# Seven block products for eight in the second expert layer's input product, with the weight preparation issued by a slot-wise feeder

## The chip, the cores and the metric

One core of a Trainium2 chip. The metric is the device time of one execution in microseconds (us), as the median of several; lower is better. TensorE does the matrix products, VectorE, ScalarE and GpSimd the elementwise work; the profile calls them PE (PEld for its weight loads), DVE, ACT and POOL. SP issues the transfers.

## The reference, cut to what matters

Local attention gives 1536 tokens of 512 features, a gated expert layer follows, and then the second one, where the change is:

```python
def _moe_ref(x, w_gate, w_val, w_out, rms_g):
    xn = x / rms * rms_g
    g = xn @ w_gate
    return (g * sigmoid(g) * (xn @ w_val)) @ w_out      # 512 -> 1536 -> 512

def _moe2_ref(x, w_in, w_out, s, b):
    h = x @ w_in                                        # 512 -> 2048
    r = np.maximum(h, 0.0)
    g = s * (r * r) + b
    return (g @ w_out).astype(np.float32)               # 2048 -> 512
```

The weights come as float64.

## The kernel before, in words

Every product of the expert layers is made of three matmuls per block of 128 x 128 weights and 512 tokens: a number is held as a high part (rounded to the matmul's fp32r format) and a low part (the rest), and high x high, low x high and high x low are summed in one PSUM bank. `mm12` (L797) does this for one strip of 128 output features and one chunk of 512 tokens: four blocks of the 512 inputs, twelve matmuls. The tokens are three chunks, s = 0, 1, 2. `banks(*range(8))` deals out the eight PSUM banks in turn, so that a bank comes back eight allocations later.

A weight strip (a "unit", 128 x 512) passes four steps, `w_load`, `w_scale`, `w_bits` and `w_split` (L222 to L279). The load brings the float64 as two 32-bit words, three buffers deep. The scale (ACT, L234) and the three word steps (DVE, L243 to L245) make a float32 of the two words in a buffer `wa`, of which there are three. The split makes the high part on ACT (L258) and the low part on POOL (L262), in rings of six. `slot(part)` (L812) is called after each product: it runs what was put off by `after(d, ...)` (a list of functions per slot ahead), one entry of `extra`, and then `w_ahead`, which moves the weight steps on by `w_to`. `next_w` hands out the next unit and, if it isn't ready, pushes it through at once. The list `order` (L190 to L200) sets the order of the stages and with it that of the units.

The first layer already has a part done with seven products for eight, `pair` (L955): two strips of the hidden features at a time, the first two token chunks as the two columns of a 2 x 2 block matrix, the third chunk in the plain way. Its derived weight blocks are units that are None in the list, made by `w_sums` (L265) from the unit before on POOL.

In the second layer, `s3(m)` (L987) does one of 16 strips of w_in2 for three chunks: 36 matmuls; for each chunk ACT makes u = relu(h) (L997), DVE s*u*u into the bank (L998), ACT the high part with the bias (L832), DVE the low part (L833). `s4(g)` (L1002) multiplies four strips' results with four rows of w_out2: 12 tiles of 128 tokens, 12 matmuls each, added to the output on DVE (L1025; the first group is copied by ACT, L1023). The last group is sent out tile by tile. The output product of the first layer, `s2(2)` (L929), adds its sum to the earlier parts (L945) and splits the result into y (`two`, L829 and L830), which is the input of s3.

Of the kernel before, what the change touches and what calls it, by code (L numbers as in the profile page):

```python
# [20 lines left out]
NPAIR = NH // 2  # L21
# [37 lines left out]
def kernel(ctx: ExitStack, tc: tile.TileContext, q_t, k_t, v_w, v_t, w_gate, w_val, w_out, w_in2, w_out2, vecs, out):  # L59
# [11 lines left out]
    xnp = pool("xn", 2)  # L71
    rawp = pool("raw", 3)
    wap = pool("wa", 3)
# [41 lines left out]
    qc = [const.tile([128, NPAIR, 2, HQ], F32, name=f"q{i}") for i in range(QB)]  # L115
# [80 lines left out]
    for m in range(KF2):  # L196
        order.append(("s3", m))
        if m % 4 == 0 and m:
            order.append(("s4", m // 4 - 1))
    order.append(("s4", KF2 // 4 - 1))  # L200
    units = []
    for kind, m in order:
        if kind == "s1":
            units += [w_gate[m], w_val[m]]
        elif kind in ("gate", "val"):
            units.append((w_gate if kind == "gate" else w_val)[m])
        elif kind == "s2":
            units += [w_out[KD * m + i] for i in range(KD)]
        elif kind == "pair":
            for q in range(2):  # L210
                units += [w_out[KD + m - PAIRS[0] + q], None]
        elif kind == "s3":
            units.append(w_in2[m])
        else:
            units += [w_out2[4 * m + i] for i in range(4)]
    NU = len(units)
    raw_t, a_t, ready = {}, {}, {}
# [4 lines left out]
    def w_load(i):  # L222
        if units[i] is None:
            return
        t = rawp.tile([128, 512, 2], I32, tag="raw", name="raw")
        fetch(out=t.rearrange("p f c -> p (f c)"), in_=units[i].bitcast(I32))
        raw_t[i] = t

    def w_scale(i):
        if units[i] is None:  # L230
# [17 lines left out]
    def w_bits(i):  # L248
        if units[i] is None:
            return  # L250
        for op in w_ops(i):
            op()
# [12 lines left out]
    def w_sums(i):  # L265

        t = sums[i + 1] = wsp.tile([128, 4, 128], F32, tag="ws", name="ws")
        a = a_t[i].rearrange("p (b c) -> p b c", b=4)
        for o, x0, x1, op in ((t[:, 0], a[:, 2], a[:, 3], ALU.add), (t[:, 1], t[:, 0], a[:, 0], ALU.subtract),
                              (t[:, 2], a[:, 0], a[:, 2], ALU.subtract), (t[:, 3], a[:, 1], t[:, 1], ALU.subtract)):  # L270
            nc.gpsimd.tensor_tensor(out=o, in0=x0, in1=x1, op=op)

    def w_split(i):
        if units[i] is None:
            a_t[i] = sums.pop(i).rearrange("p b c -> p (b c)")
        elif i + 1 < NU and units[i + 1] is None:
            w_sums(i)
        w_high(i)
        w_low(i)  # L279
# [4 lines left out]

    def w_to(*ns):
        for j in (3, 2, 1, 0):
            top = min(ns[j], prog[j - 1] if j else NU)
            if j == 0:
                top = min(top, prog[2] + 3)
            elif j == 1:  # L290
                top = min(top, prog[3] + 3)
            elif j == 3:
                top = min(top, live[0] + 6)
            while prog[j] < top:
                steps[j](prog[j])
                prog[j] += 1

    def w_ahead(part):

        i = used[0]  # L300
        if part == 0:
            w_to(i + 8, i + 7, 0, i + 5)
        elif part == 1:
            w_to(i + 8, 0, i + 6, 0)

    def next_w(keep=0):
        i = used[0]
        live[0] = i - keep
        while i not in ready:
            w_to(i + 4, i + 2, i + 2, i + 1)  # L310
        used[0] += 1
        return ready.pop(i)
# [531 lines left out]
    def moe(x, ps_m):  # L844

        gs, y = {}, []
# [81 lines left out]

        def s2(g):  # L929
            last = g > 0  # L930
            if last:
                flush()
                for s in range(NSUB):
                    y.append(xyp.tile([128, 2, KD, SUB], F32, tag="xy", name="y"))
            for m in range(KD):
                w = next_w()
                for s in range(NSUB):
                    ps = ps_m()[:, 0:SUB]
                    mm12(ps, w, lambda kk, e: hs[4 * g + kk][:, s, e])
                    slot(s)  # L940
                    acc = yp[:, m, s]
                    if not last:
                        nc.scalar.activation(out=acc, in_=ps, func=AF.Copy)
                    else:
# [42 lines left out]
        def s3(m):  # L987
            if m == 0:
                flush()
            w = next_w()  # L990
            g = gs[m] = chunk()
            for s in range(NSUB):
                ps = ps_m()[:, 0:SUB]
                mm12(ps, w, lambda kk, e: y[s][:, e, kk])
                slot(s)
                u = steady_u()
                nc.scalar.activation(out=u, in_=ps, func=AF.Relu)  # L997
                after(0, lambda u=u, ps=ps: nc.vector.scalar_tensor_tensor(out=ps, in0=u, scalar=sbc[:, 0:1], in1=u, op0=ALU.mult, op1=ALU.mult))  # L998
                after(1, lambda ps=ps, g=g[:, s]: two(ps, (g[:, 0], g[:, 1]), bbc[:, 0:1]))
            yield  # L1000

        def s4(g):  # L1002
# [3 lines left out]
            ws = [next_w(j) for j in range(4)]  # L1006
            for t in range(NT):
                st, c = divmod(t * 128, SUB)
                ge = [gs[4 * g + e][:, st, :, c:c + 128] for e in range(4)]
                parts = 2 if last and t == NT - 1 else 1  # L1010
                for k in range(parts):
                    cs = slice(k * DM // parts, (k + 1) * DM // parts)
                    acc = ps_m()[:, cs]
                    for e in range(4):
                        gh = r(ge[e][:, 0])
                        nc.tensor.matmul(acc, gh, r(ws[e][0][:, cs]), start=e == 0, stop=False)  # L1016
                        nc.tensor.matmul(acc, gh, r(ws[e][1][:, cs]), start=False, stop=False)  # L1017
                    for e in range(4):
                        nc.tensor.matmul(acc, r(ge[e][:, 1]), r(ws[e][0][:, cs]), start=False, stop=e == 3)  # L1019
                    if k == 0:  # L1020
                        slot(t % NSUB)
                    if g == 0:
                        nc.scalar.activation(out=op[:, t, cs], in_=acc, func=AF.Copy)  # L1023
                    else:
                        nc.vector.tensor_tensor(out=op[:, t, cs], in0=acc, in1=op[:, t, cs], op=ALU.add)  # L1025
                    if last:
                        nc.sync.dma_start(out=out[t * 128:(t + 1) * 128, cs], in_=op[:, t, cs])
                yield

        for kind, m in order:  # L1030
            yield from {"s1": s1, "gate": gate_of, "val": val_of, "s2": s2, "pair": pair, "s3": s3, "s4": s4}[kind](m)
# [15 lines left out]
def _layout(q, k, v, moe_w_gate, moe_w_val, moe_w_out, moe_rms_g, moe2_w_in, moe2_w_out, moe2_s, moe2_b):  # L1047
# [29 lines left out]
    def strips(w):  # L1077
# [14 lines left out]
        "w_in2": c(strips(moe2_w_in)).reshape(KF2, 128, 512),  # L1092
# [25 lines left out]
```

## Time and profile before

| | us |
|---|---|
| median of 3 runs | 637.85 (637.02 to 638.58) |
| the profiled execution | 637.69 |
| its span | 635.9 |
| TensorE busy in the span | 621.4 (98%) |
| VectorE, ScalarE, GpSimd busy | 405.9, 272.4, 200.5 |

The span is what the hardware profiler recorded on the core; the execution's own time has a little around it. The rows of the trace give busy time, count and mean duration of groups of instructions by line of the kernel, with the idle time of the engine just before them. A matmul's row shows its way through the pipeline, in which the next one has already begun. The attention and the first products take some 125 us, the first layer's rest runs to 371 us, the second layer from there to 633.

### The profile page before, as it was taken

The numbers are of one execution on the slowest core, as the hardware profiler recorded it, in microseconds if no ns is written. First come the engines' busy times: TensorE is split into PE (matmuls) and PEld (weight loads), VectorE is DVE, ScalarE is ACT, GpSimd is POOL, SyncE is SP. The second block draws the span as 40 slices with busy tenths as digits, with TensorE's granted clock in tenths as the row PEclk, the third lists the DMA queues.
The fourth block names the chain that finished last, engine by engine and source line by source line (L and its number), as shares of the span: only waits on it lengthen the run. The fifth ranks groups of instructions, "written<-read, shape, count | busy, mean of one in ns | idle before, by whom it ended". The sixth has DMA issues, their size and how long they took to land.

```text
span 635.9 us, 9741 instructions
## 1 busy us (share of the span) xinstructions
PE 621.4 (98%) x3826; PEld 511.6 (80%) x3826; DVE 405.9 (64%) x748; ACT 272.4 (43%) x547; POOL 200.5 (32%) x213
## 2 busy tenths in 40 slices
PE   5999999999999999999999999999999999999998
PEld 3877788878888888878888888888888888888886
DVE  5699884236714795799876768850588457845532
ACT  2898974324433443413343345531553055304400
POOL 2266844403414754637731101100410031103000
DMA  8897230003501131132232221140222221110022
GB/s 283 289 312 228 85 101 2 0 1 113 185 1 33 39 127 35 37 102 95 66 99 67 68 66 39 61 133 0 67 68 68 65 66 67 62 38 1 1 99 101
DMA packets 17015, 53.55 MB, mean 84 GB/s; under 512 B 1905, under 2 KB 2161, under 8 KB 16969
## 3 DMA queue, kind: packets, MB, share of 16 engines
q1 hardware_dynamic: 16968, 52.92, 25.8%
q8 instruction: 30, 0.49, 0.3%
q14 instruction: 17, 0.13, 0.1%
HBM read 48.86 MB, written 3.15 MB: 82 GB/s over the span
## 4 chain that ended last, share of the span: by engine, by line
PE 91%; DVE 4%; DMA 3%; ACT 1%; issue 1%; POOL 1%; DVEq 0%; POOLq 0%
PE b L808 20%; PE b L804 20%; PE b L805 20%; PE b L1019 7%; PE b L1016 7%; PE b L1017 7%; PE b L600 2%; PE b L656 2%; PE b L637 2%; DMA hg<-in_k_t_dram 1%; PE b L350 1%; PE b L951 1%; PE b L952 1%; PE b L953 1%; DMA q<-in_q_t_dram 1%
## 5 line engine op out<-in xcount | busy, mean ns | idle before, releaser
L262 POOL TENSOR_TENSOR wl<-wa,wh 128x512 fp32r<-128x512 f32 x68 | 90.0, 1330 | 295.1 <-ACT wh L258 259.0
L804 PE MATMUL b<-x,wh 128*128 128x512 f32 x288 | 113.7, 395 | 0.9 <-DVE u L779 0.9
L805 PE MATMUL b<-x,wl 128*128 128x512 f32 x288 | 112.2, 390 | 0.0
L258 ACT ACTIVATE wh<-wa 128x512 fp32r<-128x512 f32 x68 | 41.4, 625 | 89.3 <-PE b L1019 45.5
L808 PE MATMUL b<-x,wh 128*128 128x512 f32 x288 | 77.9, 392 | 0.0
L1017 PE MATMUL b<-wl,hg 128*128 128x512 f32 (+1 forms) x196 | 75.1, 385 | 0.0
L1016 PE MATMUL b<-wh,hg 128*128 128x512 f32 (+1 forms) x196 | 75.1, 385 | 0.0
L804 PE MATMUL b<-y,wh 128*128 128x512 f32 x192 | 74.7, 389 | 0.0
L805 PE MATMUL b<-y,wl 128*128 128x512 f32 x192 | 74.7, 389 | 0.0
L998 DVE SCALAR_TENSOR_TENSOR b<-u,vec 128x512 f32<-128x512 f32 x48 | 50.7, 1056 | 35.6 <-ACT u L997 35.6
L804 PEld LDWEIGHTS b<-x,wh 128*128 128x128 f32 x288 | 54.1, 188 | 12.4 <-issue 1.3
L805 PEld LDWEIGHTS b<-x,wl 128*128 128x128 f32 x288 | 54.1, 188 | 10.7
L808 PEld LDWEIGHTS b<-x,wh 128*128 128x128 f32 x288 | 53.5, 188 | 11.0
L245 DVE SCALAR_TENSOR_TENSOR wa<-raw,wa 128x512 int32<-128x512 int32 x68 | 56.8, 835 | 2.1
L244 DVE SCALAR_TENSOR_TENSOR wa<-raw,wa 128x512 int32<-128x512 int32 x68 | 54.6, 803 | 2.1
L833 DVE SCALAR_TENSOR_TENSOR hg<-b,vec,hg 128x512 fp32r<-128x512 f32 x48 | 36.0, 749 | 28.1 <-ACT hg L832 28.1
L1025 DVE TENSOR_TENSOR part<-b,part 128x512 f32<-128x512 f32 (+1 forms) x37 | 24.4, 674 | 43.5 <-PE b L1019 43.5
L1019 PE MATMUL b<-wh,hg 128*128 128x512 f32 (+1 forms) x196 | 51.5, 385 | 0.0
L832 ACT ACTIVATE hg<-b,vec 128x512 fp32r<-128x512 f32 x48 | 33.0, 688 | 43.0 <-DVE b L998 43.0
L808 PE MATMUL b<-y,wh 128*128 128x512 f32 x192 | 51.3, 389 | 0.0
L234 ACT ACTIVATE wa<-raw 128x512 f32<-128x512 f32 x68 | 44.4, 662 | 7.9 <-POOL wl L262 7.6
L1016 PEld LDWEIGHTS b<-wh,hg 128*128 128x128 f32 x196 | 36.8, 188 | 7.3
(116 smaller groups left out, 1072.0 us busy)
## 6 DMA issues: line engine op xcount, KB each, us to landing
raw<-in_w_out_dram SPq DMA_DIRECT2D x28, 512.0 KB, 3.6
raw<-in_w_in_dram SPq DMA_DIRECT2D x16, 512.0 KB, 3.5
raw<-in_w_gate_dram SPq DMA_DIRECT2D x12, 512.0 KB, 4.5
raw<-in_w_val_dram SPq DMA_DIRECT2D x12, 512.0 KB, 4.1
hg<-in_k_t_dram SPq DMA_DIRECT2D x8, 400.0 KB, 5.5
vt<-in_v_t_dram SPq DMA_DIRECT2D x8, 400.0 KB, 4.1
part<-in_v_w_dram SPq DMA_DIRECT2D x6, 528.0 KB, 5.9
q<-in_q_t_dram SPq DMA_DIRECT2D x12, 256.0 KB, 5.1
```

The source lines that it names most:

```text
L234: nc.scalar.activation(out=a, in_=raw_t[i][:, :, 1].bitcast(F32), func=AF.Copy, scale=2.0 ** -112)
L244: lambda: nc.vector.scalar_tensor_tensor(out=ai, in0=hi, scalar=-0x80000000, in1=ai, op0=ALU.bitwise_and, op1=ALU.bitwise_or),
L245: lambda: nc.vector.scalar_tensor_tensor(out=ai, in0=lo, scalar=29, in1=ai, op0=ALU.logical_shift_right, op1=ALU.bitwise_or),
L258: nc.scalar.activation(out=r(h), in_=a_t[i], func=AF.Copy)
L262: nc.gpsimd.tensor_tensor(out=r(lo), in0=a_t.pop(i), in1=high[i], op=ALU.subtract)
L804: nc.tensor.matmul(ps, r(hi[:, kk * 128:(kk + 1) * 128]), xh, start=kk == 0, stop=False)
L805: nc.tensor.matmul(ps, r(lo[:, kk * 128:(kk + 1) * 128]), xh, start=False, stop=False)
L808: nc.tensor.matmul(ps, r(hi[:, kk * 128:(kk + 1) * 128]), r(act(kk, 1)), start=False, stop=kk == 3)
L998: after(0, lambda u=u, ps=ps: nc.vector.scalar_tensor_tensor(out=ps, in0=u, scalar=sbc[:, 0:1], in1=u, op0=ALU.mult, op1=ALU.mult))
L1016: nc.tensor.matmul(acc, gh, r(ws[e][0][:, cs]), start=e == 0, stop=False)
L1017: nc.tensor.matmul(acc, gh, r(ws[e][1][:, cs]), start=False, stop=False)
L1019: nc.tensor.matmul(acc, r(ge[e][:, 1]), r(ws[e][0][:, cs]), start=False, stop=e == 3)
```

## The change

The strips of the second layer's w_in2 are done in pairs (`two_of`), eight of them. The inputs of a pair are 2 x 2 blocks for each half k of the inputs: two blocks of 128 input features by two strips. The first two token chunks are the other 2 x 2 matrix, and seven products, each of 2 x 3 = 6 matmuls, take the place of eight; sums of the banks (m1 is kept, u2, u3 and v are partial sums in SBUF) give the four results. The third chunk is done as before, 12 matmuls a strip. The derived blocks of the weights are units of their own, each named by the unit it comes from, and made by `w_sums` on POOL; `w_in2` is laid out anew on the host. The derived blocks of the activations (t1 to t4, and b11, b21, b22) are made by `yblocks` during the last output product of the first layer, whose last strip takes the chunks in the order 2, 0, 1. The square reads its first factor from the bank; the third chunk's low part goes to POOL.

The output products take the third chunk's tiles first, and do two strips for four tiles and then the other two, in four banks, so that only half of the weights are needed at first. From the fifth value strip of the first layer on, `feed` takes the place of `w_to` in the slots: at most one unit moves on by each step in one slot, with six `wa` buffers; from the end of the first layer on, scale and word steps stop while a pair runs (`stop`), and go on from the second half of the third chunk's tiles.

```diff
+    qp = pool("q", 1)
-    wap = pool("wa", 3)
+    wap = pool("wa", 6)
...
-    for m in range(KF2):
-        order.append(("s3", m))
-        if m % 4 == 0 and m:
-            order.append(("s4", m // 4 - 1))
-    order.append(("s4", KF2 // 4 - 1))
+    for g in range(KF2 // 4):
+        order += [("two", 2 * g), ("two", 2 * g + 1), ("s4", g)]
...
+        elif kind == "two":
+            n = len(units)
+            units += [w_in2[2 * m], w_in2[2 * m + 1], n, n + 1]
...
+    def feed():
+
+        now[0] += 1
+        for j in (3, 2, 1, 0):
+            while prog[j] < (prog[j - 1] if j else NU) and derived[prog[j]] and j < 3:
+                prog[j] += 1
+            i = prog[j]
+            if i >= (prog[j - 1] if j else NU):
+                continue
+            if j == 3 and i >= live[0] + 6 or j == 0 and real[i + 1] > real[prog[2]] + 3 or j == 1 and real[i + 1] > real[prog[3]] + 6:
+                continue
+            if j == 1 and now[0] < at.get((0, i), 0) + 3 or j == 2 and now[0] < at.get((1, i), 0) + 1:
+                continue
+            if j in (1, 2) and i >= stop[0]:
+                continue
+            if j == 1 and now[0] < at.get((3, nth[real[i] - 6]), 0) + 2:
+                continue
+            steps[j](i)
+            at[j, i] = now[0]
+            prog[j] += 1
...
+            if m == KF - 8:
+                wide[0] = 1
...
+        def yblocks(m, s, u):
+            k, j = divmod(m, 2)
+
+            def split(n, a, eng, late=0):
+                d = YB[k, n]
+                after(late, lambda: nc.scalar.activation(out=r(d[0]), in_=a, func=AF.Copy))
+                after(late, lambda: eng.tensor_tensor(out=r(d[1]), in0=a, in1=d[0], op=ALU.subtract))
+
+            yf[j, s] = u
+            e = nc.gpsimd
+            if s == 0:
+                split(("b11", "b21")[j], u, nc.vector)
+            elif j == 0:
+                t1 = yf["t1"] = steady_u()
+                e.tensor_tensor(out=t1, in0=u, in1=yf[0, 0], op=ALU.subtract)
+                split("t1", t1, e, 1)
+            else:
+                t2 = steady_u()
+                e.tensor_tensor(out=t2, in0=u, in1=yf["t1"], op=ALU.subtract)
+                nc.vector.tensor_tensor(out=yf[0, 1], in0=u, in1=yf[0, 1], op=ALU.subtract)
+                e.tensor_tensor(out=yf[1, 0], in0=yf[1, 0], in1=t2, op=ALU.subtract)
+                split("b22", u, nc.vector)
+                split("t2", t2, nc.vector)
+                split("t3", yf[0, 1], e)
+                split("t4", yf[1, 0], e)
...
+            def prod(bank, w, b, n):
+                for k in range(2):
+                    d = YB[k, n]
+                    cs = slice(b * 128, b * 128 + 128)
+                    nc.tensor.matmul(bank, r(w[k][0][:, cs]), r(d[0]), start=k == 0, stop=False)
+                    nc.tensor.matmul(bank, r(w[k][1][:, cs]), r(d[0]), start=False, stop=False)
+                    nc.tensor.matmul(bank, r(w[k][0][:, cs]), r(d[1]), start=False, stop=k == 1)
...
+            def act2(i, s, a):
+                d = g[i][:, s]
                 u = steady_u()
+                nc.scalar.activation(out=u, in_=a, func=AF.Relu)
+                after(0, lambda: nc.vector.scalar_tensor_tensor(out=a, in0=a, scalar=sbc[:, 0:1], in1=u, op0=ALU.mult, op1=ALU.mult))
+                if s == 2:
+                    after(1, lambda: nc.scalar.activation(out=u, in_=a, func=AF.Identity, bias=bbc[:, 0:1]))
+                    after(1, lambda: nc.scalar.activation(out=r(d[:, 0]), in_=u, func=AF.Copy))
+                    after(2, lambda: nc.gpsimd.tensor_tensor(out=r(d[:, 1]), in0=u, in1=d[:, 0], op=ALU.subtract))
+                else:
+                    after(1, lambda: nc.scalar.activation(out=r(d[:, 0]), in_=a, func=AF.Identity, bias=bbc[:, 0:1]))
+                    after(2, lambda: nc.vector.scalar_tensor_tensor(out=r(d[:, 1]), in0=a, scalar=bbc[:, 0:1], in1=d[:, 0], op0=ALU.add, op1=ALU.subtract))
...
+                w, k, b = {"m1": (aw, 0, "b11"), "m2": (aw, 1, "b21"), "m4": (aw, 3, "t4"), "m6": (sw, 1, "t2"),
+                           "m5": (sw, 0, "t1"), "m7": (sw, 2, "t3"), "m3": (sw, 3, "b22")}[n]
...
+                if n == "m1":
+                    nc.scalar.activation(out=m1, in_=bank, func=AF.Copy)
+                elif n == "m2":
+                    add(bank, bank, m1)
+                    act2(0, 0, bank)
+                elif n == "m6":
+                    add(u2, bank, m1)
+                elif n == "m7":
+                    add(u3, bank, u2)
...
+            turn = 'm1 m2 0 1 m6 m7 m4 m5 m3' if p == 0 else '0 m1 m2 1 m6 m7 m4 m5 m3'
...
+            for t0 in (8, 0, 4):
...
+                accs = [ps_m()[:, cs] for _ in range(4)]
+                for h in range(2):
+                    if h and t0 == 8:
+                        ws += [next_w(2), next_w(3)]
+                        stop[0] = NU
+                    for n in range(4):
+                        mms(accs[n], t0 + n, (2 * h, 2 * h + 1), cs, h == 0, h == 1)
+                        if n % 2 or t0 == 8:
+                            slot(0)
+                        if h:
+                            put(accs[n], t0 + n, cs)
```

In `turn`, "0" and "1" are the third chunk's two strips, each followed by its `act2`. m4 and m5 add u3, m3 adds v (m5's bank plus u2), and each of the three is followed by `act2`. The last group's output tiles of the first two chunks are done one by one, and the very last in two halves, as before.

## Rows read from the trace of the kernel before

**Rows 1.** The page's first part: busy us (share of the span) and instructions

```profile
span 635.9 us, 9741 instructions
## 1 busy us (share of the span) xinstructions
PE 621.4 (98%) x3826; PEld 511.6 (80%) x3826; DVE 405.9 (64%) x748; ACT 272.4 (43%) x547; POOL 200.5 (32%) x213
```

**Rows 2.** TensorE's waits: line, releaser, us in total, times, longest us

```profile
PE b L804 <- DVE u L779: 0.9, 1, 0.9
...
PE b L951 <- DVE part L976: 0.3, 1, 0.3
```

**Rows 3.** Windows: length, busy us of PE, PEld, DVE, ACT, POOL, then PEclk, DMA

```profile
446.80:479.40 32.60, 32.60 (x146) 26.99 (x145) 22.74 (x31) 17.87 (x31) 8.92 (x7) 1.00 0.20 66
479.40:512.10 32.70, 32.70 (x146) 27.09 (x145) 19.66 (x30) 6.15 (x11) 2.92 (x3) 1.00 0.20 65
...
223.00:239.00 16.00, 16.00 (x73) 13.15 (x72) 14.43 (x22) 7.05 (x12) 8.74 (x10) 1.00 0.36 121
271.00:285.00 14.00, 13.73 (x61) 11.06 (x60) 13.79 (x23) 2.62 (x5) 3.96 (x3) 1.00 0.29 94
```

**Rows 4.** The chain in order of time, one strip: start us, us, what

```profile
446.88 0.91 PE b L808 x4
...
449.60 0.91 PE b L808 x4
```

**Rows 5.** Groups by line and shape: busy us, mean ns; second layer's strips, first layer's pairs

```profile
L804 PE MATMUL b<-y,wh 128*128 128x512 f32 x192 | 74.7, 389 | 0.0
...
L953 PE MATMUL b<-hg,wh 128*128 128x512 f32 x44 | 17.1, 389 | 0.0
```

**Rows 6.** The same view, VectorE: the operations on banks

```profile
L998 DVE SCALAR_TENSOR_TENSOR b<-u,vec 128x512 f32<-128x512 f32 x48 | 50.7, 1056 | 35.6 <-ACT u L997 35.6
...
L833 DVE SCALAR_TENSOR_TENSOR hg<-b,vec,hg 128x512 fp32r<-128x512 f32 x48 | 36.0, 749 | 28.1 <-ACT hg L832 28.1
...
L1025 DVE TENSOR_TENSOR part<-b,part 128x512 f32<-128x512 f32 x35 | 23.6, 688 | 41.7 <-PE b L1019 41.7
...
L945 DVE TENSOR_TENSOR b<-b,part 128x512 f32<-128x512 f32 x12 | 8.3, 696 | 2.8 <-PE b L808 2.8
...
L976 DVE TENSOR_TENSOR part<-b,part 128x512 f32<-128x512 f32 x16 | 10.4, 677 | 0.0
```

**Rows 7.** By line: duration ns min/median/max, first and last start, VectorE

```profile
L998 DVE SCALAR_TENSOR_TENSOR b<-u,vec x48: 748/752/1804, 375.0 to 602.0; 128x512 f32<-128x512 f32 x48
...
L244 DVE SCALAR_TENSOR_TENSOR wa<-raw,wa x68: 679/693/1667, 21.0 to 582.5; 128x512 int32<-128x512 int32 x68
...
L976 DVE TENSOR_TENSOR part<-b,part x16: 673/677/684, 223.5 to 289.2; 128x512 f32<-128x512 f32 x16
```

**Rows 8.** Groups by line and shape, ScalarE

```profile
L832 ACT ACTIVATE hg<-b,vec 128x512 fp32r<-128x512 f32 x48 | 33.0, 688 | 43.0 <-DVE b L998 43.0
```

**Rows 9.** Groups by line and shape, GpSimd, and one line's spread

```profile
L262 POOL TENSOR_TENSOR wl<-wa,wh 128x512 fp32r<-128x512 f32 x68 | 90.0, 1330 | 295.1 <-ACT wh L258 259.0 <-DVE b L945 19.4 <-PE b L1019 7.2
...
L271 POOL TENSOR_TENSOR ws<-wa 128x128 f32<-128x128 f32 x8 | 3.7, 463 | 3.4 <-DVE wa L245 3.4
...
L271 POOL TENSOR_TENSOR ws<-wa,ws 128x128 f32<-128x128 f32 x4 | 2.3, 573 | 0.0
...
L885 POOL TENSOR_TENSOR hg<-hg x8: 1288/1392/1744, 197.5 to 266.5; 128x512 fp32r<-128x512 f32 x8
```

**Rows 10.** Groups by line, VectorE, 371 to 600 us: the word steps

```profile
L244 DVE SCALAR_TENSOR_TENSOR wa<-raw,wa 128x512 int32<-128x512 int32 x26 | 18.0, 692 | 0.9
L245 DVE SCALAR_TENSOR_TENSOR wa<-raw,wa 128x512 int32<-128x512 int32 x26 | 18.0, 692 | 0.9
...
L243 DVE TENSOR_SCALAR wa<-wa 128x512 int32<-128x512 int32 x26 | 10.9, 420 | 0.0
```

More of the change, by code (lines that the diff above doesn't have):

```diff
@@ L114 @@
     junk = const.tile([128, DM], mybir.dt.bfloat16, name="junk")
-    qc = [const.tile([128, NPAIR, 2, HQ], F32, name=f"q{i}") for i in range(QB)]
+    qc = [qp.tile([128, NPAIR, 2, HQ], F32, tag=f"q{i}", name="q") for i in range(QB)]
     part = const.tile([128, 2 * VT], F32, name="part")
@@ L216 @@
     NU = len(units)
+    derived = [isinstance(u, int) for u in units]
+    real = [0]
+    for d in derived:
+        real.append(real[-1] + (not d))
     raw_t, a_t, ready = {}, {}, {}
@@ L222, in w_load @@
     def w_load(i):
-        if units[i] is None:
+        if derived[i]:
             return
@@ L229, in w_scale @@
     def w_scale(i):
-        if units[i] is None:
+        if derived[i]:
             return
@@ L248, in w_bits @@
     def w_bits(i):
-        if units[i] is None:
+        if derived[i]:
             return
@@ L263, in w_low, with w_sums @@
         ready[i] = (high.pop(i), lo)
-    def w_sums(i):
-        t = sums[i + 1] = wsp.tile([128, 4, 128], F32, tag="ws", name="ws")
+    def w_sums(i, of):
+        t = sums[of] = wsp.tile([128, 4, 128], F32, tag="ws", name="ws")
         a = a_t[i].rearrange("p (b c) -> p b c", b=4)
@@ L273, in w_split @@
     def w_split(i):
-        if units[i] is None:
+        if derived[i]:
             a_t[i] = sums.pop(i).rearrange("p b c -> p (b c)")
-        elif i + 1 < NU and units[i + 1] is None:
-            w_sums(i)
+        else:
+            for k in (i + 1, i + 2):
+                if k < NU and derived[k] and units[k] == i:
+                    w_sums(i, k)
         w_high(i)
@@ L283 @@
     live = [0]
+    wide = [0]
     def w_to(*ns):
@@ L287, in w_to @@
             top = min(ns[j], prog[j - 1] if j else NU)
[L288 to L293, printed above, removed]
-            while prog[j] < top:
-                steps[j](prog[j])
-                prog[j] += 1
+            while prog[j] < top:
+                i = prog[j]
+                if j == 0 and real[i + 1] > real[prog[2]] + 3 or j == 1 and real[i + 1] > real[prog[3]] + 3:
+                    break
+                if j == 3 and i >= live[0] + 6:
+                    break
+                steps[j](i)
+                prog[j] += 1
+    now, at, stop = [0], {}, [NU]
+    nth = [i for i in range(NU) if not derived[i]]
+    def feed():
[3 more added lines that the diff above has]
+                prog[j] += 1
+            i = prog[j]
+            if i >= (prog[j - 1] if j else NU):
[8 more added lines that the diff above has]
+                continue
+            steps[j](i)
+            at[j, i] = now[0]
+            prog[j] += 1
     def w_ahead(part):
         i = used[0]
-        if part == 0:
+        if wide[0]:
+            feed()
+        elif part == 0:
             w_to(i + 8, i + 7, 0, i + 5)
@@ L934, in s2 @@
                     y.append(xyp.tile([128, 2, KD, SUB], F32, tag="xy", name="y"))
+                room()
             for m in range(KD):
                 w = next_w()
-                for s in range(NSUB):
+                for s in (2, 0, 1) if last and m == KD - 1 else range(NSUB):
                     ps = ps_m()[:, 0:SUB]
                     mm12(ps, w, lambda kk, e: hs[4 * g + kk][:, s, e])
+                    if last and m == KD - 1 and s < 2:
+                        stop[0] = 0
                     slot(s)
@@ L1005, in s4, with mms @@
                 flush()
-            ws = [next_w(j) for j in range(4)]
-            for t in range(NT):
+            ws = [next_w(0), next_w(1)]
+            def mms(acc, t, es, cs, start, stop):
                 st, c = divmod(t * 128, SUB)
[L1009 to L1027, printed above, removed]
@@ new lines, in mms @@
+                ge = [C[e][:, st, :, c:c + 128] for e in es]
+                for n, e in enumerate(es):
+                    gh = r(ge[n][:, 0])
+                    nc.tensor.matmul(acc, gh, r(ws[e][0][:, cs]), start=start and n == 0, stop=False)
+                    nc.tensor.matmul(acc, gh, r(ws[e][1][:, cs]), start=False, stop=False)
+                for n, e in enumerate(es):
+                    nc.tensor.matmul(acc, r(ge[n][:, 1]), r(ws[e][0][:, cs]), start=False, stop=stop and n == len(es) - 1)
@@ L1028, in s4 @@
                 yield
         for kind, m in order:
-            yield from {"s1": s1, "gate": gate_of, "val": val_of, "s2": s2, "pair": pair, "s3": s3, "s4": s4}[kind](m)
+            yield from {"s1": s1, "gate": gate_of, "val": val_of, "s2": s2, "pair": pair, "two": two_of, "s4": s4}[kind](m)
     x = [xs0]
```

132 lines of the change are left out of this document (115 added, 17 removed).

## The prediction

> **What bounds the kernel now.** I read the page's busy times first: TensorE is busy 621.4 us of a 635.9 us span, VectorE 405.9, ScalarE 272.4, GpSimd 200.5 [rows 1]. A busy TensorE need not be a working one, so I went to TensorE's waits: apart from the attention at the start, only two products waited, 0.9 and 0.3 us [rows 2]. The windows show one strip stage and one output stage of the second expert layer: TensorE is busy for the whole 32.6 and 32.7 us at a granted clock of 1.00 (the 2.4 GHz level), VectorE for 22.74 and 19.66, GpSimd for 8.92 and 2.92 [rows 3]. So here TensorE is the bound, and every other engine has slack. The chain in order of time gives the unit price: the four closing matmuls of two successive twelves begin at 446.88 and 449.60, so 2.72 us for 12, or 0.2267 us each [rows 4]. The 389 ns of a matmul's own row [rows 5] is its length in the pipeline, with the next one already begun, and isn't the price.
>
> **What the change removes from TensorE.** Two strips cost 2 x 3 x 12 = 72 matmuls before. After, two token chunks go through seven products of 2 blocks x 3 terms (42 matmuls), the third through 2 x 12 = 24: 66 in all. That is 6 fewer per pair of strips and 48 fewer over eight pairs, 48 x 0.2267 = **10.88 us**. The output products keep 12 matmuls per tile, in another order. A six-matmul product on one bank is not new: the first layer's pairs run so at 389 ns each, and a stretch of them, 223 to 239 us, has TensorE busy throughout with 73 matmuls, 0.219 each [rows 3, 5]. So I take no cost for starting a bank more often (nine banks per pair where there were six).
>
> **What each pair adds, per 66 x 0.2267 = 14.96 us of TensorE.**
> - VectorE: six squares, four low parts, seven block sums. The square now reads its first factor from the bank, as the low part does, so I price it by that row, 0.749 us, and not by the old square's mean of 1.056 [rows 6]. Sums into a bank cost 0.696 (m2, m4, m5, m3), into SBUF 0.677 (m6, m7, and v): 10 x 0.749 + 4 x 0.696 + 3 x 0.677 = 12.3 us; they come densest from m6 to m3, and the next twelve-matmul product lets the engine catch up. Cover: 14.96 us of products and a ring of eight banks, in which each is wanted again eight products later. The dear end is the row of operations with both inputs in SBUF, which spread from 0.752 to 1.804 [rows 7]; that is the third rival. I take the cheap one, as a sum read from a bank (673 to 684 ns over 16, GpSimd at work among them [rows 7]) is the same instruction.
> - ScalarE: at most 19 operations (four high parts, six Relus, six biased copies, two more copies for the third chunk, one copy of m1); at the dearest row, 0.688 [rows 8], 13.1 us. It fits.
> - GpSimd: a weight block set costs three subtractions or sums of 0.463 and one of 0.573, 1.96 us, and a low part 1.330 [rows 9]. The first pair of each group of two does two sets, four low parts and the third chunk's two low parts: 3.9 + 5.3 + 2.7 = 11.9 us; the second does no set, 8.0. At the dearest GpSimd price, 1.744 [rows 9], the first pair makes 3.9 + 6 x 1.744 = 14.4 us, still under 14.96.
> - Nothing is added to the DMA: the derived blocks are computed, the strips are as many bytes as before, and the loads go through the same queue with the same three buffers.
>
> **What is moved.** The word steps, 0.420 + 0.692 + 0.692 = 1.80 us for a strip in the second layer [rows 10], leave the pairs for the output products. I walked the new feeder slot by slot: it lifts its stop after the first four of sixteen slots, does at most one unit in a slot, and gets all eight units through by the stage's last slots. VectorE then has 8 x 1.80 + 12 x 0.688 (adding a tile [rows 6]) = 22.7 us in 32.6, and what runs over is not wanted before the pair after next. The same walk gives the lead of each split weight: derived blocks are issued at the last two slots of an output stage and wanted after 8.2 us of products, against two high and two low parts, 4.0 us; the second half of an output stage's weights is issued at m4 and m5 and wanted 6.8 us after the last, against three low parts, 4.0 us. The units are always in place when asked for, so the emergency path is not taken. The feeder also takes over from the fifth value strip of the first layer on; no unit there is split less than one gate strip ahead. Zero for all of it; with the cover gone, a late weight costs TensorE at most its own 1.33 us low part each time.
>
> **The seam before the first pair.** The blocks t1 to t4 of the activations are made in the first layer's last output product. Only those of its last strip can be late. After its last matmul come a VectorE sum (0.7), two GpSimd subtractions and two GpSimd low parts one after the other; at 1.39 us, the middle of such an operation [rows 9], t4 is ready after 6.3 us, and t3 after 4.9. TensorE has m1, m2 and both third-chunk products in between, 8.2 us, before m6, and comes to t3 after 9.5 and to t4 after 10.9. Cost zero, up to the first rival's 1.5 us.
>
> **The sum.** The profiled execution took 637.69 us around its span of 635.9; the median of the three runs is 637.85, 0.16 above. 637.69 - 10.88 = 626.8, and from the median 627.0. I forecast **626.9 us**.
>
> **The rivals.**
> 1. Part is given back where GpSimd queues. In the seam a whole split unit may stand ahead (1.96 + 1.74), then four operations at 1.744, with 1.4 us of sum and copy: t4 at 12.1 us against 10.9, t3 at 10.3 against 9.5, so 1.2 us; and one low part (about 1 us) late in another place. It ends at 626.9 + 2.2 = **629.1 us**. For it: GpSimd has twice the work per pair that it has now. Against: its queue is empty through most of the second layer. Chance 0.12.
> 2. The word steps overrun the output products. Their two steps with both inputs in SBUF spread from 0.69 to 1.667 us [rows 7], and GpSimd works 2 x (1.96 + 1.33) + 2 x 1.33 = 9.2 us in that stage. If all of that holds VectorE up, it has 22.7 + 9.2 = 31.9 us to do in 32.6, with 27.2 left when the stop lifts, and carries up to 4.7 us into the next pair, which would then ask 17.0 of VectorE in 14.96: 2.0 us late after each of three output stages, **633 us**. Against: the late operations feed banks wanted eight products later. Chance 0.05. The Trainium skill (SBUF — State Buffer, Who interferes with whom) says that a VectorE instruction with two SBUF inputs and a GpSimd instruction that reads SBUF shut each other out, the loser for the whole instruction. By that rule this rival's 9.2 us would be lost in full, and a pair's sums, each with one input in a bank, would lose nothing; the spread of the word step and the steady sum agree with its direction [rows 7], the full blocking is not shown.
> 3. Slower: VectorE becomes the bound inside the pairs. If its operations there are held up as the old square was, mean over median 1.056 / 0.752 = 1.40 [rows 6, 7], a pair takes 12.3 x 1.40 = 17.2 us and TensorE waits for a bank. It decides from 16.32 us, what two strips took (72 x 0.2267), on: 8 x (17.2 - 16.32) = +7.0, **645 us**. For it: GpSimd is busy 8 to 12 us of each pair. And in the first layer's second pair, where sums and word steps meet, VectorE is busy for 13.79 of 14.00 us and TensorE loses 0.27 [rows 3]. Against: that stretch holds the word steps of three strips, which these pairs don't, and the sums themselves didn't stretch [rows 7]. Chance 0.04.
> 4. The product count falls and the time doesn't, because each bank begun costs something that the twelve-matmul products hide. Three more banks per pair would have to cost 0.45 us each to eat 1.36: **637.8 us**. The first layer's pairs speak against it [rows 3]. Chance 0.03.
>
> **How the numbers follow.** The forecast keeps 0.76. A measurement of this kernel can tell about 0.2% from no change: runs differ by 1.56 us, 0.25%. Faster by more than that: the forecast, rivals 1 and 2, 0.93; same: rival 4, 0.03; slower: rival 3, 0.04. The range goes down to 625.7, if the two waits of 1.2 us go as well, and up to 629.9, rival 1 with half the runs' spread (0.8) on top; that holds the forecast and rival 1, 0.88, less what an unlisted wait may take.
>
> **What would show it.** Right: TensorE busy all through the pairs, the ends of two pairs 14.96 us apart, VectorE near 12 us and GpSimd near 12 or 8 us in one, squares at 0.75 us, no word step inside a pair, about 48 fewer matmuls. Wrong: a wait of TensorE on a GpSimd low part at m6, m7 or m4 (rival 1), word steps in a pair (2), VectorE above 15 us there and TensorE waiting for it (3), or pairs over 15 us without a wait (4).

## The result, and the profile after

The changed kernel takes **628.62 us** (628.22 to 629.92, four runs) against 637.43 (636.58 to 638.58, four runs) for the kernel before: a ratio of 0.9864 [0.9842, 0.9887]. The forecast was 626.9, the range 625.7 to 629.9: the time lies inside it, 1.7 us above the forecast. The profiled execution took 628.22 us around a span of 626.3, 9.6 us less than before.

The page's first part, against [rows 1]:

```profile
span 626.3 us, 9872 instructions
## 1 busy us (share of the span) xinstructions
PE 610.6 (97%) x3778; PEld 502.2 (80%) x3778; DVE 447.7 (71%) x790; ACT 299.4 (48%) x593; POOL 301.9 (48%) x321
```

TensorE has 48 matmuls fewer and 10.8 us less to do (621.4 - 610.6). The three other engines have more: VectorE 41.8 us, ScalarE 27.0, GpSimd 101.4. Next, the windows of the second layer, to be read against [rows 3]: the first two pairs, an output product, two more pairs, an output product. The columns are the length, then the busy time of PE, PEld, VectorE, ScalarE and GpSimd, the granted clock and the DMA share.

```profile
372.80:387.80 15.00, 15.00 (x68) 12.43 (x67) 12.53 (x15) 9.88 (x17) 12.51 (x12) 1.00 0.00 0
387.80:402.80 15.00, 15.00 (x68) 12.43 (x67) 12.08 (x20) 10.77 (x19) 8.95 (x8) 1.00 0.00 1
402.80:435.40 32.60, 32.60 (x145) 27.00 (x145) 22.13 (x32) 16.21 (x28) 11.12 (x13) 1.00 0.42 129
435.40:450.40 15.00, 15.00 (x68) 12.43 (x67) 7.03 (x11) 8.88 (x15) 11.79 (x15) 1.00 0.01 2
450.40:465.30 14.90, 14.90 (x67) 12.33 (x67) 11.45 (x19) 10.92 (x19) 7.61 (x7) 1.00 0.00 0
465.30:497.90 32.60, 32.60 (x146) 27.00 (x145) 28.21 (x42) 10.67 (x18) 13.54 (x16) 1.00 0.36 114
```

TensorE never pauses; a pair takes the 14.96 us of the forecast, where two strips took 16.32. VectorE, with 12.5 us at most in a pair, has room to spare, and the word steps are in the output products (28.21 us of VectorE in 32.6). So the second layer did what was forecast. What was not forecast is in TensorE's waits, the columns as in [rows 2]; of the view, all that comes after the attention:

```profile
PE b L1039 <- DVE part L1064: 1.1, 1, 1.1
...
PE b L836 <- DVE u L811: 0.9, 1, 0.9
...
PE b L1039 <- DVE part L1054: 0.8, 1, 0.8
```

The 0.9 is the one of before. The 1.1 and the 0.8 are new, and they lie in the **first layer's** first pair of seven products (L1039 is L951 of before). They take the place of the 0.3 of [rows 2], which was in the second pair: by these rows 1.6 us more.

The rows of the waits understate it. A wait's row begins where the last matmul's own row ends, 0.39 us after its start, while the price of that matmul is 0.2267; so the cost of a stop is read from the starts. The first pair's first matmul, the last one ahead of the longer wait, and the first matmul behind the pair (start, us, engine, line, operation, tiles, count):

```profile
217.48 0.39 PE L1039 MATMUL b<-hg,wh 128*128 128x512 f32 x1
...
227.86 0.39 PE L1041 MATMUL b<-hg,wh 128*128 128x512 f32 x1
...
235.28 0.40 PE L836 MATMUL b<-x,wh 128*128 128x512 f32 x1
```

The pair's 66 matmuls take 17.80 us (217.48 to 235.28), where they took 14.98 in the kernel before (218.56 to 233.54) and would take 14.96 at the unit price. The second pair no longer loses anything: 14.96 us, where it took 15.52. The first layer is so 2.26 us longer by the starts (2.82 - 0.56). TensorE also came to the first pair 1.08 us earlier (217.48 against 218.56), which is less than the profiles of the changed kernel and of the runs below differ among themselves (216.98 to 219.72). -10.88 + 2.26 - 1.08 = -9.70 us, beside the -9.6 of the span.

The stretch around the pair, columns as in [rows 3], first of the kernel before, then of the changed one; the third line of each is the whole of it, in which 178 matmuls were begun before and 165 now:

```profile
200.00:216.00 16.00, 16.00 (x72) 13.27 (x71) 7.55 (x12) 7.25 (x13) 6.58 (x5) 1.00 0.11 34
216.00:236.00 20.00, 20.00 (x90) 16.48 (x89) 19.65 (x27) 8.22 (x14) 12.74 (x12) 1.00 0.26 82
200.00:240.00 40.00, 40.00 (x178) 33.05 (x177) 29.88 (x41) 17.18 (x30) 22.48 (x19) 1.00 0.21 66
```

```profile
200.00:216.00 16.00, 16.00 (x72) 13.25 (x71) 14.87 (x20) 7.18 (x13) 6.64 (x5) 1.00 0.42 133
216.00:236.00 20.00, 18.07 (x78) 13.93 (x77) 19.79 (x23) 9.29 (x17) 15.86 (x14) 1.00 0.29 93
200.00:240.00 40.00, 38.07 (x165) 30.50 (x164) 38.56 (x49) 16.46 (x29) 23.68 (x18) 1.00 0.32 106
```

Before, VectorE was already full in the second stretch (19.65 of 20) but half idle ahead of it, and so it came in without arrears. Now it has little room in either (14.87 of 16, 19.79 of 20): the feeder, which has six buffers to fill and starts just here, puts four sets of word steps into the first stretch (one before). VectorE enters the pair late. Its timeline there (start, us, engine, line, operation, tiles, count):

```profile
223.65 1.27 DVE L1054 TENSOR_TENSOR part<-b,part 128x512 f32<-128x512 f32 x2
224.85 0.41 DVE L246 TENSOR_SCALAR wa<-wa 128x512 int32<-128x512 int32 x1
225.29 1.68 DVE L247 SCALAR_TENSOR_TENSOR wa<-raw,wa 128x512 int32<-128x512 int32 x1
227.01 1.67 DVE L248 SCALAR_TENSOR_TENSOR wa<-raw,wa 128x512 int32<-128x512 int32 x1
228.59 2.47 DVE L1064 TENSOR_TENSOR part<-b,part 128x512 f32<-128x512 f32 x4
```

The bank that TensorE wants at 228.25 is released by the sums of L1064, and in the queue a set of word steps stands ahead of them, two of which take 1.7 us where [rows 10] have 0.69. Steps of that length are not new (before, three in this stretch took 1.66); their number ahead of the pair is. TensorE gets the bank at 229.33:

```profile
229.33 0.50 PE L1039 MATMUL b<-hg,wh 128*128 128x512 f32 x1 [1.08 <-DVE part L1064]
```

### The profile page after: what moved, and what is told of

The parts are those of the page before. It is cut to its first block, busy times and chain, and to the rows that moved or that the text cites. A ratio compares the mean times of both kernels' runs of the same rounds, so it can differ in the third digit from the quotient of the medians.

```text
span 626.3 us, 9872 instructions
## 1 busy us (share of the span) xinstructions
PE 610.6 (97%) x3778; PEld 502.2 (80%) x3778; DVE 447.7 (71%) x790; ACT 299.4 (48%) x593; POOL 301.9 (48%) x321
## 4 chain that ended last, share of the span: by engine, by line
PE 90%; DVE 4%; DMA 2%; issue 2%; ACT 1%; POOL 0%; DVEq 0%; POOLq 0%
PE b L840 13%; PE b L836 13%; PE b L837 13%; PE b L1198 7%; PE b L1195 7%; PE b L1196 7%; PE b L1123 5%; PE b L1099 4%; PE b L1097 4%; PE b L1098 4%; PE b L1125 2%; PE b L632 2%; PE b L688 2%; PE b L669 2%; DMA hg<-in_k_t_dram 1%
## 5 line engine op out<-in xcount | busy, mean ns | idle before, releaser
L1195 PE MATMUL b<-wh,hg 128*128 128x512 f32 (+1 forms) x196 | 75.1, 385 | 0.0
L247 DVE SCALAR_TENSOR_TENSOR wa<-raw,wa 128x512 int32<-128x512 int32 x68 | 64.0, 941 | 2.1
L248 DVE SCALAR_TENSOR_TENSOR wa<-raw,wa 128x512 int32<-128x512 int32 x68 | 60.4, 888 | 2.1
L1108 DVE SCALAR_TENSOR_TENSOR b<-b,vec,u 128x512 f32<-128x512 f32 x48 | 35.9, 758 | 35.5 <-ACT u L1107 35.3
L1198 PE MATMUL b<-wh,hg 128*128 128x512 f32 (+1 forms) x196 | 58.0, 385 | 0.0
L246 DVE TENSOR_SCALAR wa<-wa 128x512 int32<-128x512 int32 x68 | 44.2, 651 | 15.7 <-ACT wa L237 15.0
L265 POOL TENSOR_TENSOR wl<-ws,wh 128x512 fp32r<-128x512 f32 x20 | 26.2, 1314 | 55.3 <-ACT wh L261 53.8
L1107 ACT ACTIVATE u<-b 128x512 f32<-128x512 f32 x48 | 28.3, 596 | 36.6 <-DVE b L1132 26.5
L1196 PEld LDWEIGHTS b<-wl,hg 128*128 128x128 f32 x196 | 36.8, 188 | 7.4
L1195 PEld LDWEIGHTS b<-wh,hg 128*128 128x128 f32 x196 | 36.8, 188 | 7.3
L1198 PEld LDWEIGHTS b<-wh,hg 128*128 128x128 f32 x196 | 36.4, 188 | 7.3
```

Of the source, the lines that this page charges most:

```text
L246: lambda: nc.vector.tensor_scalar(out=ai, in0=ai, scalar1=3, scalar2=1, op0=ALU.logical_shift_left, op1=ALU.bitwise_or),
L247: lambda: nc.vector.scalar_tensor_tensor(out=ai, in0=hi, scalar=-0x80000000, in1=ai, op0=ALU.bitwise_and, op1=ALU.bitwise_or),
L248: lambda: nc.vector.scalar_tensor_tensor(out=ai, in0=lo, scalar=29, in1=ai, op0=ALU.logical_shift_right, op1=ALU.bitwise_or),
L265: nc.gpsimd.tensor_tensor(out=r(lo), in0=a_t.pop(i), in1=high[i], op=ALU.subtract)
L1195: nc.tensor.matmul(acc, gh, r(ws[e][0][:, cs]), start=start and n == 0, stop=False)
L1198: nc.tensor.matmul(acc, r(ge[n][:, 1]), r(ws[e][0][:, cs]), start=False, stop=stop and n == len(es) - 1)
```

## The experiments

The theory: what the forecast lacks is VectorE's lag in the first layer, made by the feeder's word steps; in the second layer TensorE alone is the bound. The rivals: the second layer lost something that no wait shows (a cost of starting banks, a longer matmul), or what is missing is chance. All edits are to the changed kernel, and ratios are against the kernel before, run in turn with them on the same chip.

**The changed kernel again, twice.**

> The changed kernel once more, as the base for the others on the same chip. Both theories expect 628.6 us (0.986 of the kernel before), TensorE waiting about 1.8 us in two places of the first layer's first pair and nowhere in the second layer.

> The changed kernel, the base for the run beside it: 0.986 to 0.987 of the kernel before, two waits of together 1.8 to 1.9 us in the first layer's first pair.

Measured: 630.08 us (628.65 to 632.45, six runs), 0.9874 [0.9848, 0.99], and 628.95 (627.45 to 632.13, six runs), 0.9876 [0.9853, 0.9899]. Both profiles (spans 626.4 and 626.9) hold the loss again: from 200 to 240 us TensorE was busy for 38.10 and 38.04 of 40 us, with 165 matmuls, and the first pair took 17.78 and 17.80 us. The loss is no chance of one profile.

**The feeder takes over four strips later.**

```diff
-            if m == KF - 8:
+            if m == KF - 4:
                 wide[0] = 1
```

> The feeder takes over only after the first layer's pairs, from the ninth value strip on. Theory (the missing 1.6 us are word steps that the feeder puts into the first layer's pairs, where VectorE has no room): the waits of 1.1 and 0.8 us there shrink to the 0.3 of the kernel before, 1.6 us less than the changed kernel, 627.0 us, 0.984 of the kernel before. Rival (the waits come from the collisions of VectorE and GpSimd in that stretch, whoever issues the word steps, or from the larger set of buffers): they stay, 628.6 us.

Measured: 627.45 us (626.54 to 631.87), 0.9852 [0.982, 0.9884], span 624.7. The windows are nearly those of before again:

```profile
200.00:216.00 16.00, 16.00 (x72) 13.27 (x71) 8.46 (x12) 7.51 (x13) 8.16 (x7) 1.00 0.10 34
216.00:236.00 20.00, 20.00 (x90) 16.46 (x89) 18.75 (x27) 8.54 (x15) 12.68 (x12) 1.00 0.33 103
```

and so are the waits in the pairs (0.3 us). The first pair takes 15.01 us. But a wait appeared that the changed kernel doesn't have:

```profile
PE b L1097 <- ACT y L987: 0.6, 1, 0.6
```

It is in the seam: the second half of m2 waits for b21. At m1 TensorE is 2.75 us earlier than in the changed kernel (369.94 against 372.69), and ScalarE makes b21's high part no earlier (it starts at 372.05 against 371.93), since VectorE, whose sum comes first, works through the same list of operations there at the same times, three of them at 1.8 us. That VectorE isn't earlier fits the word steps that it didn't do ahead of the pairs and has to do after them: from 260 to 335 us it is busy for 70.57 of 75 us, 63.87 in the changed kernel. No run tests this. Part of what is regained in the first layer is so lost at the seam. The time by itself doesn't tell the two kernels apart (0.982 to 0.9884 here, 0.9848 to 0.99 for the changed kernel beside it); the traces do.

**Word steps stopped in the first layer's pairs too**, the feeder's start left as it is.

```diff
                 wa, ws = next_w(), next_w(1)
+                stop[0] = used[0]
...
                 yield
+            stop[0] = NU
```

> The feeder as in the changed kernel, but scale and word steps stop while a pair of the first layer runs, as they do in the second layer. Theory: the pairs have no word steps, so the two waits go, 1.6 to 1.8 us less, 626.9 us; some may stay if VectorE enters the first pair late from the word steps before it, 627.5. Rival (collisions, not the place of the word steps): 628.6 us.

> The kernel with the stop in the first layer's pairs once more, beside the changed kernel on the same chip, for an interval. Theory: 1.6 us under the changed kernel, 0.983 to 0.984 of the kernel before. Rival (its lead in the earlier runs was the chip's spread): no difference, 0.987.

Measured: 626.98 us (625.42 to 628.01, four runs), 0.982 [0.9793, 0.9847], and 628.55 (626.33 to 630.04, six runs), 0.9866 [0.9842, 0.9889]. In both traces no row of a wait is left in the pairs, and TensorE is busy for 39.90 and 39.89 of the 40 us from 200 on, 1.8 us more than in the changed kernel, and begins 176 matmuls there where that one begins 165. By the starts the first pair takes 15.40 and 15.36 us, 2.4 less. The window of the first of these runs shows it with VectorE at 17.42 us in place of 19.79, though the stretch ahead of it (14.90) is as full as it was:

```profile
200.00:216.00 16.00, 16.00 (x72) 13.27 (x71) 14.90 (x19) 6.97 (x13) 6.10 (x4) 1.00 0.41 133
216.00:236.00 20.00, 19.90 (x88) 16.11 (x87) 17.42 (x22) 9.17 (x17) 16.27 (x14) 1.00 0.17 53
```

This and the edit before it remove the same loss from different ends: fewer word steps ahead of the pair, or fewer within it. Common to both is that VectorE has fewer word steps to do by the time the pair's sums are due, so that the loss comes from them is shown. Lengthened steps alone don't bring it: with the stop, four of the steps ahead of the pair's sums still take 1.66 or 1.67 us, and the pair loses 0.4 us in place of 2.8. How much of the lag in the changed kernel is the number of steps and how much their length, the two edits don't separate.

The gain in the time is less certain than in the trace: against the changed kernel on the same chip the medians are 3.1 us lower once (626.98, 630.08) and 0.4 once (628.55, 628.95). The attention and the first products, which neither edit touches, differ from run to run: in the profiles of the second comparison TensorE came to the first pair at 219.72 with the stop and at 218.10 without, so that 0.9 us of the 2.4 are left in the span (626.0, 626.9). This version has the lowest median of all that were run; how much of the 2.4 us the median keeps is not settled.

**The eighth product put back**, in a bank that nobody reads: six matmuls more in each pair, nothing else.

```diff
                     act2(0, 0, bank)
+                    prod(new(), aw, 1, "b21")
```

> An eighth product in each pair: m2's six matmuls once more, into a bank of their own that nothing reads (the output is unchanged). Theory (TensorE is the bound through the whole second layer, at 0.2267 us a matmul and nothing for a bank begun): 8 x 6 x 0.2267 = 10.9 us more than the changed kernel, 639.5 us, as many matmuls as before and about the time of before plus the 1.6 us of the first layer's pair. Rivals: under 5 us more if something else (VectorE, weights) ends the pairs and the product fits into slack; over 14 us more if a bank begun has a price of 0.45 us.

Measured: 640.0 us (638.97 to 643.05), 1.0035 [1.0015, 1.0055]; span 637.3, 11.0 us more than the changed kernel, where 48 x 0.2267 is 10.9. The first two pairs:

```profile
372.80:389.10 16.30, 16.30 (x73) 13.51 (x72) 13.06 (x15) 10.01 (x17) 13.67 (x13) 1.00 0.00 0
389.10:405.50 16.40, 16.40 (x74) 13.57 (x73) 11.79 (x18) 10.89 (x19) 7.76 (x7) 1.00 0.00 1
```

The matmuls cost the full unit price, ten banks per pair cost no more than nine, and TensorE is what these stages wait for. No loss is hidden in the second layer. This kernel has as many matmuls as the one before (3826), and its median is 2.3 us longer (640.0, 637.68): about what the first layer's pairs lose, measured without the gain.

**The square with both inputs in SBUF**, as it was before; it is s*u*u either way.

```diff
-... scalar_tensor_tensor(out=a, in0=a, scalar=sbc[:, 0:1], in1=u, ...
+... scalar_tensor_tensor(out=a, in0=u, scalar=sbc[:, 0:1], in1=u, ...
```

> The square takes both factors from SBUF again, as in the kernel before; its result is the same. It then meets GpSimd's operations. Theory: squares stretch from 0.76 to over 1.1 us in the mean, VectorE goes from 12.3 to 14.5 us or more in the busier pairs and falls behind in them; the ring of banks covers most of it, 0 to 3 us, 630 us. Rival (the third of the prediction: VectorE near the bound in the pairs): 10 us more or over, 638 us. Rival (nothing is stretched): 628.6 us and squares of 0.76 us.

Measured: 628.93 us (627.99 to 632.76), 0.9866 [0.9825, 0.9908], span 625.9, no wait in the second layer. VectorE is busy for 13.20 us at most in a pair (14.5 or more was expected), and the mean square takes 0.99 us (over 1.1 was expected). The squares by line and shape, first as changed, then with this edit:

```profile
L1108 DVE SCALAR_TENSOR_TENSOR b<-b,vec,u 128x512 f32<-128x512 f32 x48 | 35.9, 758 | 35.5 <-ACT u L1107 35.3
```

```profile
L1108 DVE SCALAR_TENSOR_TENSOR b<-u,vec 128x512 f32<-128x512 f32 x48 | 47.2, 992 | 32.6 <-ACT u L1107 32.4
```

and their spread:

```profile
L1108 DVE SCALAR_TENSOR_TENSOR b<-b,vec,u x48: 748/759/759, 381.3 to 593.8; 128x512 f32<-128x512 f32 x48
```

```profile
L1108 DVE SCALAR_TENSOR_TENSOR b<-u,vec x48: 746/772/1712, 381.0 to 594.0; 128x512 f32<-128x512 f32 x48
```

With an input in a bank each of the 48 squares took 0.75 or 0.76 us, with GpSimd busy for 7.6 to 12.5 us of a pair; with both in SBUF they took up to 1.71. The pricing of the forecast by the row of the low part was right, and the operand that the change moved is what made it so; but the 0.23 us per square that it saves lies beside TensorE's work, and no gain from it shows in the time.

**Word steps not stopped in the second layer's pairs.**

```diff
-                        stop[0] = 0
+                        pass
...
-            stop[0] = used[0] + 0
```

> The opposite: the stop is taken out of the second layer, so that word steps run inside its pairs, two units in each. Theory (VectorE has 12.3 of 14.96 us in a pair): two units of 1.8 to 4 us ask 16 to 20 us of it, it falls behind by 1 to 5 us per pair and TensorE waits where the eight banks don't cover that, 0.5 us per pair or 4 us in all, 632 us. Rival (the eight banks and the output products cover it): 628.6 us, no wait of TensorE in the second layer.

Measured: 639.08 us (635.9 to 641.63, twelve runs), 1.0009 [0.999, 1.0028], span 637.4. The direction was expected, the size (4 us) not: all of the gain is gone. The waits:

```profile
PE b L1194 <- DVE hg L1114: 5.1, 3, 3.3
...
PE b L1122 <- DVE hg L1114: 1.0, 1, 1.0
```

6.1 us, on banks that still wait for VectorE's low part (L1114). In the windows around the longest, 3.30 us before 409.51 (TensorE's busy time alone, the clock, the DMA), the loss goes on when the wait is over:

```profile
404.00:409.00 5.00, 2.21 (x10) 0.94 0.33 105
409.50:415.20 5.70, 5.69 (x13) 0.50 0.23 83
415.20:420.00 4.80, 4.80 (x22) 1.00 0.00 0
```

13 matmuls in 5.7 us at a granted clock of 0.50 (the 1.2 GHz level), which take 13 x 0.2267 = 2.95 at the full one: 2.75 us more. From its first matmul to the start of the last the second layer is 10.4 us longer (260.68 against 250.27): 2.75 at the lower clock and 7.7 in the stops, more than the 6.1 of their rows. Another 0.7 us lies ahead of it (m1 at 373.43 against 372.69), which makes the 11.1 us of the span. Ahead of the longest wait (from 403.9 us on) VectorE's word steps take 0.4 to 0.7 us each: here it is their number, and not their length, that makes it late.

**A shorter lead of the split**: from the first pair of the second layer on, four units instead of six.

```diff
-            if j == 3 and i >= live[0] + 6 or ...
+            if j == 3 and i >= live[0] + lead[0] or ...
...
             if p == 0:
+                lead[0] = 4
```

> The feeder may split only four units ahead in the second layer, where it could split six. The derived blocks of a pair are then split during the pair itself, 5.4 us of products before m6 wants them, and the last two weights of the second to fourth output products find no free buffer in time and are pushed through when they are asked for. Theory (the leads of the changed kernel are needed): no wait at m6, as two high and two low parts take 4.0 us, but TensorE waits 2 to 3 us at the half of three output products, 6 to 9 us, and some at a lower clock after it, 636 us. Rival (the leads are more than is needed): 628.6 us.

Measured: 670.14 us (668.64 to 671.41), 1.05 [1.0466, 1.0534], span 666.7. The waits (lines are one or two further down than in the changed kernel):

```profile
PE b L1197 <- ACT wh L261: 9.1, 6, 2.6
PE b L1127 <- POOL wl L265: 7.9, 8, 1.8
PE b L1198 <- POOL wl L265: 5.3, 7, 1.0
```

22.3 us of waits for weights in 21 stops, and the span is 40.4 us longer. Part of the rest is that a stop costs more than its row, as in the first layer's pair; another part is the clock; how the rest divides between the two was not worked out. The clock in a stretch of second-layer work and over the whole layer (columns as before):

```profile
470.00:490.00 20.00, 15.38 (x54) 0.83 0.25 79
402.00:664.00 262.00, 240.70 (x999) 0.95 0.17 54
```

The expectation (636) was five times too small: it had left out that a pair's own first weights come late as well (L1127, eight times, once a pair), and the clock. A lead of six units in place of four is worth 40 us here: that no weight is late in the changed kernel hangs on it.

## Why the prediction was right, and where it was not

**The removal: right.** 10.88 us forecast, 10.8 in TensorE's busy time, 11.0 by putting it back. From the first matmul of the second layer to the start of the kernel's last one it is 261.16 us before (371.46 to 632.62) and 250.27 now (372.69 to 622.96), 10.89 less. The price of 0.2267 us from the closing twelves [rows 4] held for the six-matmul products too. The window of 223 to 239 us that the prediction took for a stretch of the first layer's pairs holds their first pair only up to 233.54; the pair itself, 14.98 us for 66 matmuls, says the same.

**Banks begun more often: zero, right.** The eighth product's bank showed it by itself. Rival 4 is out.

**The load of the pairs: right in the sum, and covered.** VectorE was to have 12.3 us in a pair and has 12.5 at most. GpSimd was to have 11.9 and 8.0, and has 12.5 and 8.95 in the first two. Two prices were too low where operations with both inputs in SBUF run together: from 372 us on a derived set takes 2.49 us (2 x 0.633 + 0.625 + 0.598), where [rows 9] gave 1.96, and three word steps 2.25 us, where [rows 10] gave 1.80. Neither is on the path. Here is that view, GpSimd's sums first:

```profile
L274 POOL TENSOR_TENSOR ws<-wa 128x128 f32<-128x128 f32 x26 | 16.5, 633 | 24.7 <-DVE wa L248 24.7
L274 POOL TENSOR_TENSOR ws<-ws,wa 128x128 f32<-128x128 f32 x13 | 8.1, 625 | 1.0
L274 POOL TENSOR_TENSOR ws<-wa,ws 128x128 f32<-128x128 f32 x13 | 7.8, 598 | 0.0
```

```profile
L247 DVE SCALAR_TENSOR_TENSOR wa<-raw,wa 128x512 int32<-128x512 int32 x24 | 20.7, 862 | 0.8
L248 DVE SCALAR_TENSOR_TENSOR wa<-raw,wa 128x512 int32<-128x512 int32 x24 | 17.9, 745 | 0.8
...
L246 DVE TENSOR_SCALAR wa<-wa 128x512 int32<-128x512 int32 x24 | 15.5, 646 | 3.1 <-ACT wa L237 2.4 <-POOL ws L274 0.7
```

**The word steps moved into the output products: right, with less room than forecast.** The second one had 28.21 us of VectorE in 32.6 (22.7 were forecast; the word steps' share is 18.2 instead of 14.4), and no word step lies in a pair. Rival 2 foresaw 31.9 us in that stage and 4.7 carried over; 4.4 us of VectorE's time were left free. What the move is worth the edit without the stop shows: some 10 us.

**The seam: zero, right, but by another operation than was listed.** t3 and t4 were forecast 4.9 and 6.3 us after the last product; their GpSimd low parts end at 378.67 and 380.37, 6.0 and 7.7 after it (372.7), near rival 1's price for each operation (1.74 us), and are wanted at 382.2 and 383.6. The nearest to late is b21, which the prediction passed over, as it priced only t3 and t4: the high part of its second half is ready at 372.56 and wanted by m2's fourth matmul at 374.73, the low part ends at 373.29 and is wanted by the sixth at 375.18. 1.9 us is all the slack of the seam, and TensorE waited there when it came 2.75 us earlier. For rival 1's cost here the prediction has 1.5 us in one place and 1.2, which its sum gives, in another; neither was paid.

**The feeder's take-over in the first layer: forecast at zero, and this is the step that failed.** The prediction asked whether a weight would be late there, found that none would be, and wrote "Zero for all of it". It costed what the feeder gives (the lead) and not what it asks for: three more buffers to fill are word steps on VectorE, and they fall into the stretch just ahead of the one place where VectorE had no slack. The row that says so stood in the prediction itself, 13.79 of 14.00 us busy and 0.27 us of TensorE lost [rows 3], but only as an argument on the pairs of the second layer. Price: 2.3 us by the starts of the matmuls (1.6 by the rows of the waits). 626.9 + 2.3 = 629.2, against 628.62 measured; the executions of the changed kernel alone lie 1.7 us apart.

**Rival 1** forecast 629.1, close to the time, by GpSimd's queue. It is not what happened: no matmul waits for a GpSimd operation. The range goes up to 629.9 on this rival's account, so that the time lies in it is in part luck: the loss that came stood at zero in the prediction, and was about as large as rival 1's, which didn't come. **Rival 3**, VectorE as the bound in the pairs, is refused for the changed kernel by its windows; the edit without the stop comes near it, by added word steps and not by dearer squares.

The two rows on the square show what running beside GpSimd does to an operation whose first input is moved from a bank to SBUF: 0.95 us more at the longest (1.712 against 0.759), and nothing with one input in a bank. The Trainium skill (SBUF — State Buffer, Who interferes with whom) gives the reason as a port pair that VectorE's second SBUF input and GpSimd share; these rows agree with its direction. That the loser is shut out for all of the other's instruction, as it says, is not shown: GpSimd's shorter operations last 0.46 us and its longer ones 1.29, and no square got longer by 1.29.

## What to carry to other kernels

A step that prepares data further ahead is to be costed twice: by when its result is there, and by what it makes other engines do in the stretch where it catches up. Look for the one stretch where that engine already has no room (here 19.65 of 20 us) and ask what comes ahead of it; an engine that goes in late stays late, and the matmul engine pays when the ring of banks has run out. And a wait of TensorE is not priced by the length of its row: count from start to start of the matmuls around it, and look at the granted clock in the microseconds behind it.

## What the runs showed of the hardware that was not expected

After a single wait of 3.30 us TensorE ran for 5.7 us at a granted clock of 0.50, and that cost another 2.75 us; waits of 0.8 to 1.1 us in the first layer's pair did not do so (1.00 in that stretch). With 22.3 us of waits of up to 2.6 us strewn over the second layer the clock had a mean of 0.95 there, and the span grew by 40.4 us.

A stop costs more than its wait even at the full clock: between the starts at 227.86 and 229.33 lie 1.47 us, 1.24 over the price of a matmul, for a wait of 1.08, and the pair's two waits of 1.9 us in all made it 2.8 us longer.

Operations on GpSimd are lengthened too where they run beside VectorE's with both inputs in SBUF, but by less: in the seam a 128 x 512 low part takes 1.74 us, 1.29 elsewhere (0.45 more; VectorE's there take 1.78 in place of 0.69). A block sum takes 0.46 us or, on the mean of the second layer, 0.63.
